# Layer 1 of a float32 network: the second matrix of three token tiles by seven block products, and the second layer's weights converted at a closer spacing

## The chip, the cores and the metric

The kernel runs on one core of one Trainium2 chip. The metric is the device time of one execution in microseconds. Before the change it is 1191.9 us, the median of three runs (1191.66 to 1201.35).

A core has these engines, each with its own in-order stream of instructions: TensorE (PE: matmuls, and loads of the stationary operand, shown as PEld), VectorE (DVE), ScalarE (ACT), GpSimd (POOL) and SyncE (SP), which here issues all DMAs. They wait for each other by semaphores. PE writes to PSUM, 8 banks of 128 partitions x 512 float32; all else lies in SBUF or, for parked data, in DRAM.

## What is computed

```python
y  = irfft(rfft(x, axis=1) * F)                 # x: 2 x 3008 x 256 -> 6016 tokens of 256
h  = y @ w_in;  x1 = (h * sigmoid(h)) @ w_out   # layer 1: 256 -> 2048 -> 256
g  = x1 @ w_gate                                # layer 2: 256 -> 1536 -> 256
out = (g * sigmoid(g) * (x1 @ w_val)) @ w_out2
```

All inputs are float32 (the weights arrive as 64-bit floats and are converted on the chip). The change touches layer 1's second product and the preparation of layer 2's weights.

## The kernel before, in words

**Split operands.** PE multiplies 128x128 blocks of weights (stationary) with up to 512 columns of data (moving). A float32 value is kept as a high and a low part, both in the type that PE takes at full rate; a product of two values is three matmuls (high x high, high x low, low x high: `PARTS`). So each operand costs an ACT cast (high) and a subtraction on DVE or POOL (low).

**Layer 1** (lines 774 to 1046) works on tiles of 512 tokens (the twelfth has 384). A *unit* is one tile t and one block f of 128 of the 2048 hidden features; there are 192, and from tile 2 on tile t holds units 16t to 16t+15. A unit does, in this order: whatever the table `todo` has for its number (weights to convert, transforms of the next tile: `s4`); `m1_in` (L527): six matmuls of 512 columns into an `h1` bank (L509), a Silu on ACT to `u` (L536), `split` (L514): high by ACT (L516), low by DVE (L517); then `drain(18)` (L1044), which issues matmuls that were queued by earlier units until 18 are left; then `m1_out` (L541), which queues this unit's six matmuls of the second matrix (L553). So the second matrix runs three units behind the first. It adds into two PSUM banks for the whole tile, and at the tile's last unit ACT copies each bank once (L559) and SP stores it to `d3`, where layer 2 reads it.

**Layer 2's weights** (`weights2`, L811): for each third q of the features and each of gate, value and output ("g", "v", "o2"), two halves are loaded and converted from 64 bits: `conv_0` (two ACT operations), `conv_a` (three on DVE: L403, L404, L407), `conv_b` (POOL, L413, 512 wide), `conv_c` (ACT high L421, POOL low L422). For "g" and "v" sums of blocks follow: `comb_a` (four POOL operations of 256 columns), `comb_b`, `comb_c` (casts on ACT, lows on POOL: L449, L454, L466, stores). Each step stands in `todo` at its own unit; `conv_c` stands one unit behind its `conv_b`. One such group starts every 11 units from unit 80 on.

**Layer 2** (`Pair`, L665) already uses seven products of blocks in place of eight, with 384 columns each, and a last matrix with 256 columns (L751) between them.

Buffers: `mp` has 35 of 4 KB, shared by nearly all; `tp` four (tile `u`); PSUM eight banks from one pool.

Of the kernel before, what the change touches and what calls it, by code (L numbers as in the profile page):

```python
# [94 lines left out]
def fft_filter_mlp_kernel(  # L95
# [681 lines left out]
    begin = {}  # L777
    for i, (l, t, _) in enumerate(units):
        begin.setdefault((l, t), i)
    todo = {}  # L780

    def at(i, fn, *args):
        todo.setdefault(i, []).append((fn, args))
# [32 lines left out]
            at(i + 8, comb_b, key, q)  # L816
            at(i + 10, comb_c, key, q)

    i = 80
    for q in range(3):  # L820
        for key in ("g", "v", "o2"):
            weights2(i, key, q)
            i += 11
    LAST = i - 3
    at(LAST, conv_s.close)

    def room():
# [274 lines left out]
```

## Time and profile before

| | |
|---|---|
| time, median of 3 runs | 1191.9 us |
| time of the profiled execution | 1192.8 us |
| its span, first to last instruction | 1191.0 us |
| granted TensorE clock | 0.998 of full speed |
| busy: PE, DVE, ACT, POOL | 1177.8, 728.0, 666.9, 432.4 us |

The page lists busy time by engine, then the chain of work that ended last, followed back from the end. Groups name the source line, the engine, the operation and the tiles (output<-inputs). Matmuls overlap: the shown length of one is longer than its distance to the next, so the cost of a matmul on PE is read from runs of equal ones, start to start. A wait is shown with what ended it.

### The profile page before, as it was taken

What the parts mean: (1) busy time and instruction counts of PE and PEld (TensorE: products, weight loads), DVE (VectorE), ACT (ScalarE), POOL (GpSimd) and SP (SyncE); (2) the same over time, 40 slices, a digit from 0 to 9 for tenths busy, and PEclk for the clock granted to TensorE, in tenths of its full rate; (3) what the DMA queues carried; (4) which work ended last, traced back from release to release, by engine and by line L of the source; (5) the groups of instructions that cost most, each with busy time, mean ns of one, the idle gap of its engine ahead of it and who ended that gap; (6) DMA issues with size and microseconds to landing.
All of it is one profiled execution on the core that took longest, in us unless ns stands there. A gap on an engine that the chain in (4) does not pass through costs nothing.

```text
span 1191.0 us, 17735 instructions
## 1 busy us (share of the span) xinstructions
PE 1177.8 (99%) x6646; PEld 1059.6 (89%) x6646; DVE 728.0 (61%) x1078; ACT 666.9 (56%) x1208; POOL 432.4 (36%) x341
## 2 busy tenths in 40 slices
PE   9899999999999999999999999999999999999998
PEld 7478788888888888888899999999999999999997
DVE  4878866763332533443345776767677676767765
ACT  4678765655565565566554454545545455454553
POOL 2547632420043244234311424334343343434332
PEclk9999999999999999999999999999999999999999
DMA  9972523323033332313573514342331434223230
GB/s 219 280 209 71 154 77 106 97 72 98 1 106 121 101 108 93 127 45 106 174 259 125 199 55 161 105 142 89 107 130 66 159 107 142 89 90 137 72 134 23
DMA packets 67574, 141.57 MB, mean 119 GB/s; under 512 B 5568, under 2 KB 32704, under 8 KB 67488
## 3 DMA queue, kind: packets, MB, share of 16 engines
q1 hardware_dynamic: 67488, 140.44, 37.0%
q8 instruction: 52, 0.85, 0.3%
q14 instruction: 34, 0.28, 0.1%
HBM read 104.50 MB, written 35.91 MB: 118 GB/s over the span
## 4 chain that ended last, share of the span: by engine, by line
PE 95%; DVE 1%; ACT 1%; DMA 1%; POOL 1%; SPq 0%; issue 0%; POOLq 0%; DVEq 0%; ACTq 0%
PE h L509 21%; PE acc L553 21%; PE acc L751 16%; PE y L616 13%; PE xa L616 8%; PE xb L616 8%; PE s L342 2%; PE s L178 2%; PE s L175 2%; DMA fr<-in_fr_dram 1%; PE s L229 1%; PE turn L247 0%; DMA zt<-d 0%; POOL w L422 0%; SPq L195 0%; POOL m L413 0%
## 5 line engine op out<-in xcount | busy, mean ns | idle before, releaser
L751 PE MATMUL acc<-w,h 128*128 128x256 f32 x1692 | 466.3, 280 | 1.9 <-DVE h L712 0.8
L751 PEld LDWEIGHTS acc<-w,h 128*128 128x128 f32 x1692 | 316.3, 188 | 3.0 <-DVE h L712 1.1
L517 DVE TENSOR_TENSOR h<-u,h 128x512 fp32r<-128x512 f32 (+1 forms) x192 | 168.6, 883 | 242.1 <-ACT h L516 241.8
L553 PE MATMUL acc<-h,w 128*128 128x512 f32 (+1 forms) x1152 | 293.2, 387 | 0.3 <-DVE h L517 0.2
L509 PE MATMUL h<-xh,w 128*128 128x512 f32 (+1 forms) x768 | 269.6, 392 | 0.6 <-POOL w L422 0.6
L553 PEld LDWEIGHTS acc<-h,w 128*128 128x128 f32 x1152 | 215.6, 188 | 44.5 <-DVE h L517 0.8
L536 ACT ACTIVATE u<-h 128x512 f32<-128x512 f32 (+1 forms) x192 | 112.6, 587 | 132.3 <-PE h L509 131.7
L616 PE MATMUL y<-xo,wst 128*128 128x384 f32 (+1 forms) x576 | 174.5, 336 | 0.0
L616 PE MATMUL xb<-xo,wst 128*128 128x384 f32 (+1 forms) x576 | 174.0, 335 | 0.0
L509 PEld LDWEIGHTS h<-xh,w 128*128 128x128 f32 x768 | 144.2, 188 | 30.2 <-POOL w L422 1.1
L616 PE MATMUL xa<-xo,w 128*128 128x384 f32 (+1 forms) x576 | 164.1, 335 | 0.0
L659 POOL TENSOR_TENSOR c<-u,s 128x384 f32<-128x384 f32 (+1 forms) x96 | 98.4, 1025 | 176.8 <-DVE u L656 138.3
L736 POOL TENSOR_TENSOR h<-c,h 128x768 fp32r<-128x768 f32 (+1 forms) x47 | 85.8, 1826 | 176.9 <-ACT h L735 173.8
L509 PE MATMUL h<-xl,w 128*128 128x512 f32 (+1 forms) x384 | 149.3, 389 | 0.0
L516 ACT CAST h<-u 128x512 fp32r<-128x512 f32 (+1 forms) x192 | 117.5, 612 | 6.2
L616 PEld LDWEIGHTS y<-xo,wst 128*128 128x128 f32 x576 | 107.3, 188 | 0.7 <-DVE u L647 0.2
L616 PEld LDWEIGHTS xb<-xo,wst 128*128 128x128 f32 x576 | 107.5, 188 | 0.0
L616 PEld LDWEIGHTS xa<-xo,w 128*128 128x128 f32 x576 | 101.5, 188 | 0.0
L709 ACT CAST h<-ga 128x768 fp32r<-128x768 f32 (+1 forms) x48 | 39.5, 823 | 100.7 <-DVE ga L707 98.4
L663 DVE TENSOR_TENSOR c<-y,s 128x384 f32<-128x384 f32 (+1 forms) x96 | 52.1, 543 | 71.4 <-PE y L616 71.4
L509 PEld LDWEIGHTS h<-xl,w 128*128 128x128 f32 x384 | 72.2, 188 | 14.7
L712 DVE TENSOR_TENSOR h<-ga,h 128x768 fp32r<-128x768 f32 (+1 forms) x47 | 70.3, 1496 | 21.4 <-ACT h L709 21.4
(104 smaller groups left out, 1493.9 us busy)
## 6 DMA issues: line engine op xcount, KB each, us to landing
wst<-ds_g SPq DMA_DIRECT2D x48, 512.0 KB, 3.5
wst<-ds_v SPq DMA_DIRECT2D x48, 512.0 KB, 3.5
raw<-in_w_out_dram SPq DMA_DIRECT2D x14, 512.0 KB, 7.8
zt<-d SPq DMA_DIRECT2D x16, 384.0 KB, 5.0
x<-in_xp_dram SPq DMA_DIRECT2D x15, 384.0 KB, 10.0
d<-z SPq DMA_DIRECT2D x11, 512.0 KB, 3.6
d<-x SPq DMA_DIRECT2D x22, 256.0 KB, 2.2
out_dram<-ob SPq DMA_DIRECT2D x21, 256.0 KB, 2.2
```

Source lines behind the costliest of these rows:

```text
L509: nc.tensor.matmul(ps[:, :n], wt[key, f // 4, g][:, wpart, o:o + P], x[xpart][:, g, :n], start=(g == 0 and k == 0), stop=(g == 1 and k == 2),)
L516: nc.scalar.copy(h[:, 0, :n], u[:, :n])
L517: nc.vector.tensor_tensor(h[:, 1, :n], u[:, :n], h[:, 0, :n], op=ALU.subtract)
L536: nc.scalar.activation(u[:, :n], ps[:, :n], AF.Silu)
L553: nc.tensor.matmul(a[:, :n], w[:, wpart, o:o + 128], h[:, xpart, :n], start=(f == 0 and k == 0), stop=(f == 15 and k == 2),)
L616: nc.tensor.matmul(o, w_op(u, key, n, wpart), x[:, xpart, :size2(t) // 2], start=(first and k == 0), stop=(last and k == 2), skip_group_ch ...
L659: nc.gpsimd.tensor_tensor(self.c[:, self.n:], u3, self.s[:, 1], op=ALU.add)
L663: nc.vector.tensor_tensor(self.c[:, :self.n], self.y, self.s[:, 0], op=ALU.add)
L709: nc.scalar.copy(h[0], a[:, :m])
L712: eng.tensor_tensor(h[1], a[:, :m], h[0], op=ALU.subtract)
L736: nc.gpsimd.tensor_tensor(h[1], c, h[0], op=ALU.subtract)
L751: nc.tensor.matmul(a[:, D * (i % 2):D * (i % 2) + D], h[hpart][:, P * i:P * i + P], w[:, wpart, f % 2], start=(at_ == 0 and k == 0 and i % ...
```

## The change

For tiles 8 to 10 (units 128 to 175; `SEVEN`) the second matrix is done pair by pair of feature blocks. A pair of two f (256 features), 256 outputs and 512 tokens is a 2x2 by 2x2 product of blocks of 128x128 with 256 columns. In place of eight block products it does seven, of sums and differences of blocks: seven times three matmuls of 256 columns, where before it was twelve of 512.

- **Weights.** `sum_a` and `sum_b` make four sums per pair (`ws1`, split into `wst`) for 8 pairs, at units 80 to 117: on POOL one operation of 512 columns, four of 128, one of 512; one ACT cast; one store to `ds1`. `load_s1` fetches a pair's 512 KB before use, 24 times.
- **Data.** `seven_in` replaces `split`. After the odd f: two differences on POOL (`t13`), two on DVE (`t24`), four casts and four lows, spread by `behind` over the three units that follow (`step2`, `step3`), so that their engines get them after the next units' own work.
- **Products.** `seven_out` queues 21 matmuls per pair; `drain(31)` at even and `drain(21)` at odd units issue 11 and 10 of them. They add into four PSUM banks: seven results of 256 columns.
- **End of a tile.** `seven_end` adds the seven results to four blocks: two copies of 256 columns on ACT, seven operations of 256 columns on DVE, two stores to `d3`.
- **Spacing.** `weights2` starts at unit 68 and every 7 units, no more at 80 and every 11, so that it ends at about unit 129. Pools open and close at other units.
- In tile 11 `drain` leaves more in the queue at first.

```diff
+SEVEN = range(8, 11)
...
         else:
             ps = psum("h1")
             mm_in(ps, "i1", f, xt_of[t], n)
+        if t in SEVEN:
+            seven_in(begin[1, t] + f, t, f, ps)
+            return
         u = tp.tile([P, 512], F32, tag="u", name="u")
...
+    def sum_a(p):
+        w = wt["o1", p // 2, p % 2].bitcast(F32)
+        s = sums1[p] = mid([P, 2, 4, P], "ws1")
+        sub = lambda o, a, b: nc.gpsimd.tensor_tensor(o, a, b, op=ALU.subtract)
+        v = s[:, 0].rearrange("p o f -> p (o f)")
+        nc.gpsimd.tensor_tensor(v, w[:, 0], w[:, 1], op=ALU.add)
+        a11, a21, a12, a22_ = (s[:, 0, i] for i in range(4))
+        nc.gpsimd.tensor_tensor(s[:, 1, 0], a21, a22_, op=ALU.add)
+        sub(s[:, 1, 1], s[:, 1, 0], a11)
+        sub(s[:, 1, 2], a11, a21)
+        sub(s[:, 1, 3], a12, s[:, 1, 1])
...
+        def step2():
+            low(x2, flat(u))
+            t24 = new("t24")
+            sub(nc.vector, t24[:, 0], u[:, 1], t13[:, 0])
+            sub(nc.vector, t24[:, 1], t24[:, 0], u[:, 0])
+            x13 = operand(5, 7, t13)
+
+            def step3():
+                low(x13, flat(t13))
+                x24 = operand(6, 4, t24)
+                behind(i + 3, low, x24, flat(t24))
+
+            behind(i + 2, step3)
+
+        behind(i + 1, step2)
...
+        block = {1: 0, 2: 2, 4: 3}
+        order = (1, 2, 5, 3, 7, 6, 4)
...
+        queue.extend((one, i, k) for i in range(7) for k in range(3))
+
+    def seven_end(t, i, a):
...
+        if i == 0:
+            nc.scalar.copy(e[:, 0], a[:, 0])
+            add(c[:, 0, 0], a[:, 1], e[:, 0])
+        elif i == 1:
+            nc.scalar.copy(e[:, 1], a[:, 0])
+            add(e[:, 2], a[:, 1], e[:, 1])
+        elif i == 2:
+            add(e[:, 0], a[:, 1], e[:, 0])
+            add(e[:, 3], a[:, 0], e[:, 0])
+            add(c[:, 0, 1], e[:, 2], e[:, 0])
+            add(c[:, 1, 1], e[:, 3], e[:, 1])
...
+        else:
+            add(c[:, 1, 0], e[:, 3], a[:, 0], ALU.subtract)
...
-    i = 80
+    i = 68
     for q in range(3):
         for key in ("g", "v", "o2"):
             weights2(i, key, q)
-            i += 11
-    LAST = i - 3
-    at(LAST, conv_s.close)
+            i += 7
+    LAST = 176
...
+    for p in range(8):
+        at(80 + 5 * p, sum_a, p)
+        at(82 + 5 * p, sum_b, p)
+    for t in SEVEN:
+        for p in range(8):
+            at(begin[1, t] + 2 * p - 4, load_s1, t, p)
...
-            m1_in(*units[i][1:])
-            drain(6 * (LAG - 1))
-            m1_out(*units[i][1:])
+            t, f = units[i][1:]
+            if t in SEVEN:
+                m1_in(t, f)
+                settle(i)
+                drain(31 if f % 2 == 0 else 21)
+                if f % 2:
+                    seven_out(t, f // 2)
+                continue
+            m1_in(t, f)
+            settle(i)
+            drain(max(6 * (LAG - 1), 33 - 6 * f) if t > SEVEN[-1] else 6 * (LAG - 1))
+            m1_out(t, f)
```

**PE, in tiles 8 and 9.** Before, every unit is six matmuls of the first matrix and six of the second (one unit of tile 8; `w` is a half of a block of weights, and a row says how many equal ones follow each other):

```order
L509 MATMUL h1_4264<-xh_3489,w_1204 128x512
L509 MATMUL h1_4264<-xl_3490,w_1204 128x512
L509 MATMUL h1_4264<-xh_3489,w_1204 128x512
L509 MATMUL h1_4264<-xh_3489,w_1267 128x512
L509 MATMUL h1_4264<-xl_3490,w_1267 128x512
L509 MATMUL h1_4264<-xh_3489,w_1267 128x512
L553 MATMUL acc_4064<-h_4179,w_1084 128x512 x3
```

Now a pair of f takes two units; six more matmuls follow behind these rows. `b11` is the high and low of the pair's first block of data, the `h` the other blocks, `w` a block of the weights, `wst` a sum of blocks, the four `acc` the four banks:

```order
L641 MATMUL acc_4336<-b11_4651,w_1402 128x256 x3
L641 MATMUL acc_4336<-h_4683,w_1402 128x256 x3
L641 MATMUL acc_4343<-h_4716,wst_4504 128x256 x3
L641 MATMUL acc_4343<-h_4683,wst_4504 128x256 x2
L512 MATMUL h1_4793<-xh_4155,w_541 128x512
L512 MATMUL h1_4793<-xl_4156,w_541 128x512
L512 MATMUL h1_4793<-xh_4155,w_541 128x512
L512 MATMUL h1_4793<-xh_4155,w_678 128x512
L512 MATMUL h1_4793<-xl_4156,w_678 128x512
L512 MATMUL h1_4793<-xh_4155,w_678 128x512
L641 MATMUL acc_4343<-h_4683,wst_4504 128x256
L641 MATMUL acc_4368<-h_4716,wst_4504 128x256 x3
```

The twelve matmuls of 512 columns of a pair have become 21 of 256, cut in two by the next unit's first matrix.

**DVE, where tile 8 ends and tile 9 begins** (units 144 to 147). Before, a tile's end has nothing on DVE; between the low halves (L517) stand only steps of the conversion:

```order
L517 TENSOR_TENSOR h_4340<-u_4338,h_4340 128x512
L517 TENSOR_TENSOR h_4362<-u_4360,h_4362 128x512
L403 TENSOR_SCALAR v2_4349<-v2_4349 128x512
L404 TENSOR_SCALAR v2_4349<-v2_4349 128x512
L407 SCALAR_TENSOR_TENSOR v2_4349<-raw_4311,v2_4349 128x512
L517 TENSOR_TENSOR h_4385<-u_4383,h_4385 128x512
L517 TENSOR_TENSOR h_4404<-u_4402,h_4404 128x512
```

Now (L577 is a low half, L595 a difference, L653 `seven_end`, `acc` a PSUM bank of tile 8, `e1` and `x2` its results):

```order
L577 TENSOR_TENSOR b11_4769<-u0_4767,b11_4769 128x256
L577 TENSOR_TENSOR h_4775<-t13_4739,h_4775 128x512
L653 TENSOR_TENSOR e1_4784<-acc_4343,e1_4784 128x256
L653 TENSOR_TENSOR e1_4784<-acc_4368,e1_4784 128x256 x2
L653 TENSOR_TENSOR x2_4785<-e1_4784 128x256 x2
L653 TENSOR_TENSOR x2_4785<-e1_4784,acc_4375 128x256
L577 TENSOR_TENSOR h_4805<-u1_4800,h_4805 128x512
L595 TENSOR_TENSOR t24_4844<-u1_4800,t13_4802 128x256
L595 TENSOR_TENSOR t24_4844<-t24_4844,u1_4800 128x256
L577 TENSOR_TENSOR h_4809<-t24_4772,h_4809 128x512
L577 TENSOR_TENSOR b11_4841<-u0_4839,b11_4841 128x256
```

Six operations of `seven_end` stand in one block ahead of the low half of `u`, the two differences `t24`, and the low half of the pair before (`t24_4772`).

**POOL, around unit 100.** Before, at units 99 to 107, these operations are all that POOL is given there (L449 and L454 `comb_b`, L466 `comb_c`, L413 `conv_b`, L422 `conv_c`):

```order
L449 TENSOR_TENSOR wa_3258<-v2_3050,wa_3258 128x512
L454 TENSOR_TENSOR wa2_2993<-v2_3050,wa2_2993 128x256
L466 TENSOR_TENSOR wst_3311<-ws_3217,wst_3311 128x4x128
L466 TENSOR_TENSOR wst_3315<-ws_3217,wst_3315 128x4x128
L413 TENSOR_TENSOR m_3319<-m_3319,e_3320 128x512
L422 TENSOR_TENSOR w_3387<-m_3319,w_3387 128x512
L413 TENSOR_TENSOR m_3391<-m_3391,e_3392 128x512
L422 TENSOR_TENSOR w_3460<-m_3391,w_3460 128x512
```

Now, at units 100 to 104 (L416 `conv_b`, L425 `conv_c`, L439 and L440 `comb_a`, L553, L555 and L557 `sum_a`, L566 `sum_b`):

```order
L416 TENSOR_TENSOR v2_3302<-v2_3302,e_3386 128x512
L555 TENSOR_TENSOR ws1_3445<-w_1092 128x512
L557 TENSOR_TENSOR ws1_3445<-ws1_3445 128x128
L553 TENSOR_TENSOR ws1_3445<-ws1_3445 128x128 x3
L425 TENSOR_TENSOR w_3471<-v2_3302,w_3471 128x512
L440 TENSOR_TENSOR ws_3496<-v2_3302 128x256
L439 TENSOR_TENSOR ws_3496<-ws_3496,v2_3302 128x256
L439 TENSOR_TENSOR ws_3496<-v2_3302 128x256
L439 TENSOR_TENSOR ws_3496<-v2_3302,ws_3496 128x256
L566 TENSOR_TENSOR wst_3505<-ws1_3445,wst_3505 128x4x128
L452 TENSOR_TENSOR wa_3550<-v2_3302,wa_3550 128x512
```

Eight operations in nine units have become thirteen in five, seven of them for the sums of layer 1's blocks; two more of units 103 and 104 follow.

## Rows read from the trace of the kernel before

**Rows 1.** The page: busy time by engine; the chain that ended last, by engine.

```profile
PE 1177.8 (99%) x6646; PEld 1059.6 (89%) x6646; DVE 728.0 (61%) x1078; ACT 666.9 (56%) x1208; POOL 432.4 (36%) x341
...
PE 95%; DVE 1%; ACT 1%; DMA 1%; POOL 1%; SPq 0%; issue 0%; POOLq 0%; DVEq 0%; ACTq 0%
```

**Rows 2.** Stretches: start:end in us, then as the header row says.

```profile
core 0: us, PE busy (x) PEld busy (x) DVE busy (x) ACT busy (x) POOL busy (x), PEclk, DMA share, GB/s
100.00:125.00 25.00, 25.00 (x109) 19.98 (x109) 21.94 (x20) 20.50 (x36) 18.46 (x11) 1.00 0.35 90
319.00:459.00 140.00, 140.00 (x644) 115.75 (x642) 57.94 (x89) 84.78 (x153) 49.19 (x43) 1.00 0.31 98
459.00:597.00 138.00, 138.00 (x632) 114.10 (x631) 52.29 (x81) 83.60 (x148) 48.81 (x42) 1.00 0.35 116
```

**Rows 3.** Timeline of PE: start us, us, instruction; runs of equal matmuls.

```profile
466.93 1.53 PE L553 MATMUL acc<-h,w 128*128 128x512 f32 x6
...
1180.61 1.48 PE L751 MATMUL acc<-w,h 128*128 128x256 f32 x11
```

**Rows 4.** Timeline of ACT: the Silu of units 80, 128 and 176.

```profile
319.43 0.60 ACT L536 ACTIVATE u<-h 128x512 f32<-128x512 f32 x1 [1.48 <-PE h L509]
...
458.97 0.60 ACT L536 ACTIVATE u<-h 128x512 f32<-128x512 f32 x1 [1.48 <-PE h L509]
...
597.31 0.49 ACT L536 ACTIVATE u<-h 128x384 f32<-128x384 f32 x1 [1.18 <-PE h L509]
```

**Rows 5.** Groups by line and form: count | busy us, mean ns | idle before.

```profile
L516 ACT CAST h<-u 128x512 fp32r<-128x512 f32 x176 | 109.3, 621 | 5.7
...
L536 ACT ACTIVATE u<-h 128x512 f32<-128x512 f32 x176 | 104.8, 595 | 117.7 <-PE h L509 117.1
...
L422 POOL TENSOR_TENSOR w<-v,w 128x512 fp32r<-128x512 f32 x12 | 15.6, 1296 | 23.0 <-ACT w L421 23.0
...
L466 POOL TENSOR_TENSOR wst<-ws,wst 128x512 fp32r<-128x512 f32 x12 | 15.3, 1293 | 24.2 <-ACT wst L465 24.2
...
L407 DVE SCALAR_TENSOR_TENSOR v<-raw,v 128x512 uint32<-128x512 uint32 x12 | 8.3, 693 | 0.4
...
L403 DVE TENSOR_SCALAR v<-v 128x512 f32<-128x512 f32 x12 | 5.0, 420 | 0.0
...
L454 POOL TENSOR_TENSOR wa<-v,wa 128x256 fp32r<-128x256 f32 x6 | 4.4, 738 | 0.0
...
L761 DVE COPY ob<-acc 128x256 f32<-128x256 f32 x3 | 1.3, 423 | 1.4 <-ACT ob L759 1.1 <-PE acc L751 0.3
...
L759 ACT COPY ob<-acc 128x256 f32<-128x256 f32 x2 | 0.7, 370 | 2.0 <-PE acc L751 2.0
```

**Rows 6.** Timeline of DVE and POOL: low halves alone, and meeting a POOL operation.

```profile
201.36 1.27 POOL L295 TENSOR_TENSOR y<-y,t2t 128x512 f32<-128x512 f32 x1 [5.15 <-DVE t2t L291]
201.76 1.42 DVE L517 TENSOR_TENSOR h<-u,h 128x512 fp32r<-128x512 f32 x1 [0.55 <-ACT h L516]
...
205.65 0.69 DVE L517 TENSOR_TENSOR h<-u,h 128x512 fp32r<-128x512 f32 x1 [0.46 <-ACT h L516]
...
481.81 2.39 DVE L517 TENSOR_TENSOR h<-u,h 128x512 fp32r<-128x512 f32 x2
482.04 1.61 POOL L413 TENSOR_TENSOR m<-m,e 128x512 uint32<-128x512 uint32 x1 [5.00 <-DVE m L407]
```

**Rows 7.** Waits of ACT from 100 to 220 us: total, times, longest.

```profile
ACT w L421 <- POOL m L413: 9.4, 6, 2.0
```

**Rows 8.** DMA issues: count, KB each, us to landing.

```profile
wst<-ds_g SPq DMA_DIRECT2D x48, 512.0 KB, 3.5
```

More of the change, by code (lines that the diff above doesn't have):

```diff
@@ L136, in fft_filter_mlp_kernel @@
     }
+    ds1 = [dr.tile([P, 1024], F32, name=f"ds1_{p}") for p in range(8)]
     dw2 = [dr.tile([P, 1024], F32, name=f"dw2_{q}") for q in range(3)]
@@ new lines, in sum_b, with load_s1, high, low @@
+    def sum_b(p):
+        c = sums1.pop(p)[:, 1]
+        w = mid([P, 4, 2, P], "wst", F32R)
+        nc.scalar.copy(w[:, :, 0], c)
+        nc.gpsimd.tensor_tensor(w[:, :, 1], c, w[:, :, 0], op=ALU.subtract)
+        store(ds1[p], w.rearrange("p o l f -> p (o l f)"))
+    def load_s1(t, p):
+        w = wt["s1", t, p] = mid([P, 4, 2, P], "wst", F32R)
+        nc.sync.dma_start(w.rearrange("p o l f -> p (o l f)").bitcast(F32), ds1[p])
+    def high(o, v):
+        nc.scalar.copy(o[:, 0], v)
+    def low(o, v):
+        nc.vector.tensor_tensor(o[:, 1], v, o[:, 0], op=ALU.subtract)
@@ new lines, in seven_in, with operand @@
+    def seven_in(i, t, f, ps):
+        p, j = divmod(f, 2)
+        new = lambda name: spp["p"].tile([P, 2, 256], F32, tag="s", name=name)
+        flat = lambda v: v.rearrange("p i n -> p (i n)")
+        u = new(f"u{j}")
+        nc.scalar.activation(flat(u), ps, AF.Silu)
+        if j == 0:
+            b11 = tp.tile([P, 512], F32, tag="u", name="b11").bitcast(F32R)
+            b11 = b11.rearrange("p (l n) -> p l n", l=2)
+            high(b11, u[:, 0])
+            hs["u"], hs[t, p] = u, {1: b11}
+            behind(i + 1, low, b11, u[:, 0])
+            return
+        u0, x = hs.pop("u"), hs[t, p]
+        sub = lambda e, o, a, b: e.tensor_tensor(o, a, b, op=ALU.subtract)
+        def operand(k0, k1, v):
+            h = mid([P, 2, 512], "h", F32R)
+            high(h, flat(v))
+            x[k0], x[k1] = h[:, :, :256], h[:, :, 256:]
+            return h
+        t13 = new("t13")
+        sub(nc.gpsimd, t13[:, 0], u0[:, 1], u0[:, 0])
+        sub(nc.gpsimd, t13[:, 1], u[:, 1], u0[:, 1])
+        x2 = operand(2, 3, u)
+        def step2():
[10 more added lines that the diff above has]
+        behind(i + 1, step2)
@@ new lines, in seven_out, with one @@
+    def seven_out(t, p):
+        w, ws = wt["o1", p // 2, p % 2], wt.pop(("s1", t, p))
+        x = hs.pop((t, p))
+        block = {1: 0, 2: 2, 4: 3}
+        order = (1, 2, 5, 3, 7, 6, 4)
+        def one(i, k):
+            n = order[i]
+            if k == 0 and p == 0 and i % 2 == 0:
+                acc[1, t, i // 2] = psum("acc")
+            a = acc[1, t, i // 2]
+            wpart, xpart = PARTS[k]
+            if n in block:
+                left = w[:, wpart, P * block[n]:P * block[n] + P]
+            else:
+                left = ws[:, {5: 0, 6: 1, 7: 2, 3: 3}[n], wpart]
+            nc.tensor.matmul(
+                a[:, 256 * (i % 2):256 * (i % 2) + 256], left, x[n][:, xpart],
+                start=(p == 0 and k == 0 and i % 2 == 0), stop=(p == 7 and k == 2),
+                skip_group_check=True,
+            )
+            if p == 7 and k == 2 and (i % 2 or i == 6):
+                seven_end(t, i // 2, a.rearrange("p (i n) -> p i n", i=2))
+        queue.extend((one, i, k) for i in range(7) for k in range(3))
@@ L779, in fft_filter_mlp_kernel, with behind @@
         begin.setdefault((l, t), i)
-    todo = {}
+    todo, post = {}, {}
+    def behind(i, fn, *args):
+        post.setdefault(i, []).append((fn, args))
     def at(i, fn, *args):
@@ L1038, in fft_filter_mlp_kernel, with settle @@
         at(1, conv_c, "o1", 0, 1)
+        def settle(i):
+            for fn, args in post.pop(i, ()):
+                fn(*args)
         for i in range(len(units)):
```

18 lines of the change are left out of this document (16 added, 2 removed).

## The prediction

> **What bounds the kernel now.** The page comes first: PE is busy 1177.8 of 1191.0 us, and 95% of the chain that ended last is PE [rows 1]. The stretches come next. From 319 to 597 us, where the change works, PE is busy all the time, DVE for about 40%, ACT for 60%, POOL for 35% [rows 2]. So PE sets the end there, and a matmul less is time saved unless PE then has to wait. Last come single operations and how they meet, which decide whether PE will wait. The unit's pace is read from the Silu: unit 80 at 319.43 us, unit 128 at 458.97, unit 176 at 597.31 [rows 4]: 2.91 and 2.88 us per unit.
>
> **Part 1: PE's saving.** A run of six matmuls of 512 columns shows 1.53 us [rows 3]. The last one's own shown length is 0.39, so the distance is (1.53 - 0.39) / 5 = 0.228 us. A run of eleven of 256 columns, each with its own weight load as in the change, shows 1.48 us with 0.28 for the last: 1.20 / 10 = 0.120 [rows 3]. A pair costs 12 x 0.228 = 2.74 us before and 21 x 0.120 = 2.52 after. The 24 pairs save 24 x 0.22 = 5.2 us. If 256 columns cost half of 512 (0.114) they would save 24 x 0.34 = 8.2; the run measured is the nearest row, so I take 5.2 and let the range go up to 6.5.
>
> **Part 2: a steady pair.** It takes 2 x 6 x 0.228 + 2.52 = 5.26 us on PE. ACT gets two Silu (0.60), four casts of 512 or less (0.62) [rows 5]: 3.7 us. DVE gets three lows of 0.69 [rows 6], one low and two differences of 256 columns. For those no row stands; 0.35 (half of 0.69) and 0.42 (256 columns out of PSUM, [rows 5]) bound them, I take 0.40. That is 3.3 us. POOL gets two differences of 256 columns at 0.74 [rows 5]. Nothing is full. The tightest operand is the low half of x24: DVE has it some 3.7 us after the pair's second Silu could start, while PE first needs it behind 10 products, a first matrix, 11 products, a first matrix and 5 products, 5.9 us. Spare: about 2 us. I cost the steady pair at nothing; its cover is that spare and the matmuls that run three units behind.
>
> **Part 3: the ends of tiles.** In unit 145 and 161 the last products of a tile are issued, and `seven_end` gives DVE a block of six operations ahead of the low half of u, the two differences and the low half of x24. Let T be the moment when PE has issued that unit's first matrix. ACT can start the Silu 0.2 us later (a matmul is shown 0.39 long at 0.23 distance), and does Silu 0.60, two casts 0.62 each, then the copy out of PSUM 0.37 [rows 5]: T + 2.4. Only then can the block start: four operations out of PSUM at 0.42, two in SBUF at 0.40, 2.5 us: T + 4.9. Then 0.69 + 0.80 + 0.69: T + 7.1. PE wants it after 10 x 0.12 + 1.37 + 11 x 0.12 + 1.37 + 5 x 0.12 = T + 5.9. PE waits 1.2 us, and two POOL differences fall into that time, each of which can hold a DVE operation up for its 0.74 (part 4): I add 0.7. So 1.9 us, twice. At the end of tile 10 the next units are ordinary ones with 384 columns, and their cast and low half stand ahead of the pair's steps: 0.2 + 0.49 [rows 4] + 0.52 + 0.55 (a cast and a low of 384 by their rows of 512, scaled a little down), then 0.69 + 0.80 + 0.69, 3.9 us, against 9 x 0.12 + 6 x 0.17 + 7 x 0.12 = 2.9 on PE: 1.0 us. Together 2 x 1.9 + 1.0 = 4.8 us; from 0 (if DVE's copies come sooner than I think) to 7.
>
> **Part 4: the weights closer together.** POOL and DVE hold each other up. A low half takes 0.69 us alone; one that starts 0.40 us into a POOL operation takes 1.42 and ends 0.55 us after that operation. The other way round, a POOL operation that starts 0.23 us into a low half takes 1.61 in place of about 1.28, and the next low half again ends 0.55 us after it [rows 6]. So one of the two works at a time, and their times add. The Trainium skill says the same ("SBUF — State Buffer", Who interferes with whom): a DVE operation with two inputs in SBUF and a GpSimd operation that reads SBUF exclude each other for a whole instruction. By the rule every operation counts in full against one budget; if the two only slowed each other a little, this part would cost nothing, as POOL alone then fits.
>
> The sum for units 76 to 125, 50 units of 2.91 = 145.5 us. By the new table POOL gets 61 operations of 512 columns at 1.29, 26 of 256 at 0.74 [rows 5], and 32 of 128 (no row; 0.46 by the straight line through the other two): 112.6 us. DVE adds 50 low halves at 0.55 and 14 `conv_a`: the last of its three operations reads two inputs (0.69 [rows 5], 0.55 held), the other two read one and count between 0 and 0.42 [rows 5]. That is 27.5 + 7.7 + 0 to 11.8. Total 147.8 to 159.6, so 2 to 14 us more than there is room for; I take 8. What is behind hangs on POOL. Its `conv_b` releases ACT's cast in `conv_c`, and behind that cast in ACT's order stand the Silu and the high half that PE needs. A unit's result is wanted three units later, 8.7 us, and its own chain takes 2 to 3 us: 5.5 to 6.5 us may be lost unseen, and 2.9 more since `conv_c` is a unit behind `conv_b`. Against this stands a stretch that is about as full: from 100 to 125 us DVE is busy 21.9 of 25, ACT 20.5, POOL 18.5, and PE all the time [rows 2]; ACT waited for POOL there 9.4 us, at most 2.0 at once [rows 7]. An overrun of 8 is just about covered, one of 14 is not. I take 2.5 us, from 0 to 10.
>
> The rest costs nothing: 24 loads and 8 stores of 512 KB are issued eight units (over 20 us) before use, against 3.5 us to landing [rows 8], and DMA is at 0.35 of its time [rows 2]; SP's queue waits for buffers that have long been read. Tile 8's first units issue only first matrices, and catch up on the queue two units later; the queue only grows. Layer 2's loads find its weights earlier in DRAM than before.
>
> **Sum.** -5.2 + 4.8 + 2.5 = +2.1 us on the profiled execution's 1192.8. That is 0.9 above the median, so against the median 1191.9 + 2.1 = 1194.0.
>
> **Rivals.**
> 1. *Everything is hidden*: DVE runs far enough ahead at the ends of tiles, and the conversion fits. Only part 1 is left: 1191.9 - 5.2 = 1186.7, down to 1185.5 with the upper saving. For it: no wait of PE shows in these 278 us, though all operands are made on the run. Against it: the block at a tile's end starts from a copy that comes after three other ACT operations.
> 2. *The conversion takes over* (the other side): POOL and DVE together become the bound in units 76 to 125, and PE follows their pace. Price: the whole overrun of 14 less some 3 that stay unseen, since each wait of ACT also delays what it would have fed; 1191.9 - 5.2 + 4.8 + 11 = 1202.5, up to 1206. It decides from an overrun of about 9 us on. For it: by single operations the sum is over the room in any case. Against it: 100 to 125 us.
> 3. *256 columns do not cost half of 512*: each product's weight load sets the distance. The break-even is 2.74 / 21 = 0.130 us. The Trainium skill speaks against the change here ("TensorE: Matmul & The Clock Gate", Back-to-back issue gap): it gives about 81 ns for 128 columns and 131 ns for 512 in a stream of loads and matmuls, by which small products are dear; by a straight line 256 would cost 98, and a pair 2.06 in place of 1.57 us. No such thing shows here: 512 columns take 0.228, 256 take 0.120. If the distance in the new runs were 0.140, a pair would lose 0.2 us, and the time be 1191.9 + 4.8 + 4.8 + 2.5 = 1204.0.
>
> **How the numbers follow.** My forecast, 1190 to 1198, has 0.60; rival 1 0.17; rival 2 0.18; rival 3 0.03; something not thought of 0.02. The predicted time is that of the first, 1194.0. The range goes from rival 1's 1186.0 to 1202.0, which takes in the lower part of rival 2 and leaves out some 0.17. A measurement of this kernel can tell about 1% from no change, 11.9 us. Faster than 1180.0 is in no case: 0.01. Slower than 1203.8 are the upper part of rival 2 and rival 3: 0.11. The rest, 0.88, is within 1%.
>
> **What would show it.** Runs of products (L641) at 0.120 us: part 1 right. PE waiting for DVE's low half (L577) about 2 us once near the start of tiles 9 and 10 and 1 us at tile 11, and at no other place in tiles 8 to 10: parts 2 and 3 right; a wait in every pair would break part 2. In units 80 to 130 POOL busy above 85%, ACT waiting for POOL in `conv_c` (L424) for several us at once, and PE short by 0 to 10 us: part 4. No wait of ACT above 3 us there would make rival 1's half of it true.

## The result and the profile after

The changed kernel took 1213.6 us (median of 6 runs, 1206.6 to 1217.1) against 1195.1 for the kernel before, measured beside it (1191.7 to 1201.4): a ratio of 1.0138, 95% interval 1.0093 to 1.0184. It is slower by about 1.4%. The forecast of 1194.0 and its range of 1186.0 to 1202.0 were wrong.

The profiled execution took 1213.7 us. Where the difference lies is read from the Silu, as in [rows 4]. These are the Silu of units 68 and 191 in the timeline of ACT, before (283.53 and 630.20 us) and after:

```profile
283.53 0.60 ACT L536 ACTIVATE u<-h 128x512 f32<-128x512 f32 x1 [0.55 <-PE h L509]
630.20 0.49 ACT L536 ACTIVATE u<-h 128x384 f32<-128x384 f32 x1 [1.07 <-PE h L509]
```

```profile
289.05 0.60 ACT L542 ACTIVATE u<-h 128x512 f32<-128x512 f32 x1 [0.55 <-PE h L512]
651.05 0.49 ACT L542 ACTIVATE u<-h 128x384 f32<-128x384 f32 x1 [1.07 <-PE h L512]
```

Before, these 123 units took 346.7 us; after, 362.0: **15.3 us more**. Layer 2 behind them takes 560.8 us in both. Ahead of them the profile after is 5.5 us late, all of it before unit 0, where the two kernels do the same: that is scatter, since unit 0's Silu lies anywhere from 71.6 to 78.7 us in the profiles of this study, at 78.7 in a kernel whose program up to there is that of before. So kernels are compared below by the time of these 123 units, beside their ratios.

The page after, busy time by engine, beside [rows 1], and the waits of PE from 280 to 640 us (what waited and for whom: total us, times, longest):

```profile
PE 1183.0 (98%) x6862; PEld 1070.3 (88%) x6862; DVE 812.6 (67%) x1195; ACT 687.5 (57%) x1264; POOL 518.2 (43%) x437
```

```profile
PE acc L641 <- DVE h L577: 5.6, 4, 1.6
PE h L512 <- DVE xl L359: 2.8, 2, 2.3
PE s L345 <- DMA zt<-d: 2.4, 2, 2.0
PE acc L687 <- DVE h L520: 2.1, 4, 1.0
PE acc L641 <- ACT h L574: 0.7, 1, 0.7
PE acc L687 <- ACT h L519: 0.4, 1, 0.4
```

The kernel before has no such line in these units. Only the first and the fifth belong to the seven products (L641); the others lie before 478 us, in the units in which the weights are converted and the sums made. Where PE loses is read from the start of each unit's first matrix in the timeline of PE. These are units 68 and 128, before and after:

```profile
281.93 0.39 PE L509 MATMUL h<-xh,w 128*128 128x512 f32 x1
457.41 0.39 PE L509 MATMUL h<-xh,w 128*128 128x512 f32 x1
```

```profile
287.46 0.39 PE L512 MATMUL h<-xh,w 128*128 128x512 f32 x1
472.50 0.39 PE L512 MATMUL h<-xh,w 128*128 128x512 f32 x1
```

So after needs 185.0 us where before needs 175.5: PE has lost 9.6 us when unit 128 begins. Read in the same way it has lost 12.2 at unit 132, and 4.2 more in units 132 and 133, which issue the products of tile 8's first pair (beside early_sums, below, whose seven products begin without any loss). The saving less the tile ends makes -1.1, as in early_sums. Together that is the 15.3.

A part of these losses is clock. After two of the long waits PE got half of its clock; the stretches (the eighth number is the granted clock, as in [rows 2]) are the one behind the wait for zt, the next one, and the one behind the waits of tile 8's first pair:

```profile
405.50:408.50 3.00, 3.00 (x8) 2.31 (x8) 2.93 (x5) 2.05 (x5) 2.29 (x2) 0.50 1.01 345
409.00:412.00 3.00, 3.00 (x15) 2.44 (x14) 0.55 (x1) 1.26 (x3) 2.27 (x3) 1.00 0.78 309
491.50:494.20 2.70, 2.70 (x10) 2.22 (x9) 2.67 (x5) 1.49 (x4) 1.29 (x1) 0.51 0.88 287
```

That is 1.2 in place of 2.4 GHz: at 406.93 us a run of six matmuls of 512 columns shows 2.42 us in place of the 1.53 of [rows 3]. It costs some 1.5 us each time, and is part of the 12.2 and of the 4.2.

**How ACT comes to stand.** The timelines of POOL, of ACT, of DVE and of PE around 350 us:

```profile
344.93 2.79 POOL L469 TENSOR_TENSOR wst<-ws,wst 128x512 fp32r<-128x512 f32 x2 [1.49 <-ACT wst L468]
347.69 1.47 POOL L555 TENSOR_TENSOR ws<-w 128x512 f32<-128x512 f32 x1
349.23 0.79 POOL L557 TENSOR_TENSOR ws<-ws 128x128 f32<-128x128 f32 x1
350.10 2.07 POOL L553 TENSOR_TENSOR ws<-ws 128x128 f32<-128x128 f32 x3
352.13 1.27 POOL L416 TENSOR_TENSOR m<-m,e 128x512 uint32<-128x512 uint32 x1
```

```profile
345.90 0.62 ACT L519 CAST h<-u 128x512 fp32r<-128x512 f32 x1
...
347.06 0.62 ACT L519 CAST h<-u 128x512 fp32r<-128x512 f32 x1
353.44 0.62 ACT L424 CAST w<-m 128x512 fp32r<-128x512 f32 x1 [5.76 <-POOL m L416]
353.96 0.62 ACT L565 CAST wst<-ws 128x512 fp32r<-128x512 f32 x1
354.49 0.59 ACT L542 ACTIVATE u<-h 128x512 f32<-128x512 f32 x1
```

```profile
345.05 1.52 DVE L406 TENSOR_SCALAR m<-m 128x512 f32<-128x512 f32 x1
346.60 1.40 DVE L407 TENSOR_SCALAR m<-m 128x512 uint32<-128x512 uint32 x1
348.04 1.67 DVE L410 SCALAR_TENSOR_TENSOR m<-raw,m 128x512 uint32<-128x512 uint32 x1
349.63 1.80 DVE L520 TENSOR_TENSOR h<-u,h 128x512 fp32r<-128x512 f32 x2
```

```profile
350.63 1.41 PE L687 MATMUL acc<-h,w 128*128 128x512 f32 x5 [0.72 <-DVE h L520]
```

ACT finishes a high half at 347.7 us and then stands at the cast of `conv_c` (L424), which needs `conv_b` (L416). DVE is done with `conv_a` at 349.7, held up itself by POOL. But POOL first makes two low halves of `comb_c` (L469) and a whole `sum_a` (L553 to L557), and comes to L416 at 352.1. (With `sum_b` a pair's sums are six operations on POOL; the section on the change says seven.) Behind the cast stands the Silu of unit 87, whose first matrix PE began at 342.58: it runs at 354.49, 11.9 us later, where before it is 1.6.

The last link to PE is mostly DVE. PE's wait at 350.63 is for the first of the two low halves at 349.63. ACT had its high half ready at 346.52, but DVE was in `conv_a` until 349.71, with three operations of 4.6 us that take 1.5 where POOL is idle. Of PE's 7.7 us of waits before 478 us, 4.9 are for DVE, 2.4 for zt and 0.4 for ACT. So here PE waits because ACT was late already and DVE, held up by POOL, added to it.

### The profile page after: what moved, and what is told of

It reads as the page before. It is cut to its first block, busy times and chain, and to the rows that moved or that the text cites. A ratio compares the mean times of both kernels' runs of the same rounds, so it can differ in the third digit from the quotient of the medians.

```text
span 1211.9 us, 18548 instructions
## 1 busy us (share of the span) xinstructions
PE 1183.0 (98%) x6862; PEld 1070.3 (88%) x6862; DVE 812.6 (67%) x1195; ACT 687.5 (57%) x1264; POOL 518.2 (43%) x437
## 4 chain that ended last, share of the span: by engine, by line
PE 58%; DVE 2%; POOL 2%; issue 1%; ACT 1%; POOLq 0%; DVEq 0%
PE acc L885 16%; PE y L750 12%; PE xa L750 8%; PE xb L750 8%; PE h L512 6%; PE acc L641 4%; PE acc L687 2%; PE s L345 1%; DVE h L577 0%; POOL w L425 0%; POOL m L416 0%; DVE h L520 0%; DVE x L653 0%; POOL wst L566 0%; POOL v L416 0%
## 5 line engine op out<-in xcount | busy, mean ns | idle before, releaser
L520 DVE TENSOR_TENSOR h<-u,h 128x512 fp32r<-128x512 f32 (+1 forms) x144 | 143.7, 1008 | 138.7 <-ACT h L519 133.7
L687 PE MATMUL acc<-h,w 128*128 128x512 f32 (+1 forms) x864 | 221.8, 387 | 2.9 <-DVE h L520 2.4
L687 PEld LDWEIGHTS acc<-h,w 128*128 128x128 f32 x864 | 161.9, 189 | 38.1 <-DVE h L520 4.9
L542 ACT ACTIVATE u<-h 128x512 f32<-128x512 f32 (+1 forms) x144 | 83.9, 582 | 47.1 <-PE h L512 45.0
L519 ACT CAST h<-u 128x512 fp32r<-128x512 f32 (+1 forms) x144 | 87.7, 609 | 4.6
```

The lines of the kernel that those rows point to most:

```text
L519: nc.scalar.copy(h[:, 0, :n], u[:, :n])
L520: nc.vector.tensor_tensor(h[:, 1, :n], u[:, :n], h[:, 0, :n], op=ALU.subtract)
L687: nc.tensor.matmul(a[:, :n], w[:, wpart, o:o + 128], h[:, xpart, :n], start=(f == 0 and k == 0), stop=(f == 15 and k == 2),)
```

## The experiments

All ratios are to the kernel before on the same chip. The table puts together what the sections below read: the time of units 68 to 191 against the 346.7 of before; what PE has lost by the start of unit 128; then, in the stretch from the Silu of unit 76 to that of unit 126 (its ends in whole us), its length, the busy time of POOL and of ACT, and ACT's waits for anybody but PE (the view of waits, summed), all in us.

| kernel | ratio [95%] | 68 to 191 | by 128 | length | POOL | ACT | ACT's waits |
|---|---|---|---|---|---|---|---|
| before | | 0 | 0 | 148 | 48.5 | 89.3 | 11.2 |
| after | 1.0138 [1.0093, 1.0184] | +15.3 | 9.6 | 164 | 130.4 | 103.0 | 59.2 |
| close_alone | 0.9999 [0.9983, 1.0015] | 0.0 | 0.0 | 147 | 86.1 | 100.0 | 30.9 |
| close_and_sums | 1.0087 [1.0062, 1.0111] | +10.0 | 8.9 | 163 | 131.0 | 103.6 | 57.6 |
| no_unused_split | 0.9997 [0.9981, 1.0014] | -1.1 | 0.0 | 147 | 118.3 | 98.9 | 27.7 |
| no_unused_pool | 1.0077 [1.0054, 1.0101] | +8.6 | 3.9 | 157 | 118.7 | 102.4 | 52.8 |
| no_unused_act | 1.0053 [1.0035, 1.0072] | +5.3 | 1.8 | 154 | 130.9 | 98.3 | 48.5 |
| early_zt | 1.0121 [1.0096, 1.0147] | +14.4 | 9.1 | 163 | 130.7 | 102.7 | 58.6 |
| early_sums | 0.9995 [0.9973, 1.0018] | -1.1 | 0.0 | 147 | 86.0 | 100.1 | 28.6 |
| later_cast | 1.0104 [1.0075, 1.0132] | +12.3 | 7.2 | 162 | 135.9 | 102.6 | 53.9 |
| half_sums | 1.0052 [1.0032, 1.0073] | +7.0 | 2.7 | 157 | 110.3 | 100.8 | 52.7 |
| sums_on_dve | 0.9997 [0.9976, 1.0018] | +1.0 | 0.6 | 151 | 103.0 | 103.1 | 41.7 |

### Which part of the change costs the time

**wide_again**, the old spacing put back:

```diff
-    i = 68
+    i = 80
-            i += 7
+            i += 11
```

> The changed kernel with only the old spacing of the second layer's weights put back (unit 80, step 11); sums of weights and seven products stay. Theory (POOL and DVE have more work in units 76 to 125 than the stretch is long, and PE is held through it): POOL's 9 conversions spread over 99 units again, so the overrun goes; left are the saving of 5.8 us and the tile ends of 4.5 us: 0.995 to 1.003 of the kernel before. Rival A (the seven products themselves cost the time): stays at 1.010 to 1.018. Rival B (the start before unit 0 was really made slower by the change, 5.5 us in its profile): Silu of unit 0 at 77 to 79 us here too.

Measured: 1.0170 [1.0148, 1.0191]; units 68 to 191 take 22.3 us more. The theory's forecast fell, and the number lies in rival A's range. Up to unit 128 nothing is lost (Silu of unit 68 to that of 128: 175.4 us, as before), as the theory says; but the conversion now runs through tiles 8 to 10, and there PE waits in many pairs for the operands of the seven products (waits of PE, 280 to 640 us):

```profile
PE acc L641 <- DVE h L577: 19.9, 17, 2.6
```

So the spare 2 us of a steady pair hold only while POOL and DVE have no conversion to do: the closer spacing is not an extra of this change but what its products need. That they cost the time by themselves, as rival A has it, falls with early_sums below, which keeps them and loses nothing. Rival B fell too: unit 0's Silu is at 71.6 us here.

**close_alone**, the kernel before with the closer spacing alone:

```diff
-    i = 80
+    i = 68
-            i += 11
+            i += 7
-    LAST = i - 3
+    LAST = 176
```

> The kernel before with only the spacing changed (unit 68, step 7); no sums of weights, no seven products. Theory: without the sums POOL and DVE have some 36 us less to do in units 76 to 125 (147.8 to 159.6 becomes about 112 to 123 against 145.5 us of room), so nothing is late: 0.999 to 1.003. Rival A: the same, 1.000. Rival C (the spacing alone does it, by ACT's casts or SP's queue of loads and stores): 1.007 or more.

Measured: 0.9999 [0.9983, 1.0015], and no wait of PE in these units. The closer spacing by itself is free.

**close_and_sums**, the changed kernel with no tile computed by seven products:

```diff
-SEVEN = range(8, 11)
+SEVEN = range(0)
...
-            drain(max(6 * (LAG - 1), 33 - 6 * f) if t > SEVEN[-1] else 6 * (LAG - 1))
+            drain(6 * (LAG - 1))
```

> The changed kernel with its seven products taken out: units of tiles 8 to 10 as before, weights at step 7, and the sums of weights made and stored but read by nobody. Theory: the overrun in units 76 to 125 is all there and the saving is not: 1.008 to 1.014, the waits of PE at the same places as in the changed kernel between 349 and 475 us, some 10 to 12 us of them. Rival A: 0.999 to 1.003, PE without such waits.

Measured: 1.0087 [1.0062, 1.0111], +10.0 us, as the theory had it, with PE's starts too far apart at the places of the kernel after (by 0.85 us at 347.8, 1.14 at 391.1, 1.86 at 399.0, 0.89 at 470.2, and half clock from 403.6 on). (The 24 loads of the sums, from unit 124 on, are left out here too.) So the sums in units 80 to 117, with the conversions, cost about 10 of the 15.3 us. The seven products add 5.4 to that: -1.1 for their saving less the tile ends, 4.2 at the first pair of tile 8, which ACT and DVE enter late, and 2.3 close ahead of it (the last wait for xl is 2.5 us at 472.5 in the kernel after, 0.9 here).

**no_unused_split.** The trace of ACT's waits led to `conv_c`: for g and v nobody reads what it makes.

```diff
         v, _ = parts.pop((key, q, half))
+        if key in ("g", "v"):
+            return
```

> The changed kernel without conv_c for the keys g and v: 12 casts on ACT and 12 low halves on POOL whose results nobody reads (comb_b splits the same numbers again). Theory: POOL has 12 x 1.29 = 15.5 us less in units 76 to 125, 132 to 144 against 145.5 us of room, the overrun goes: 0.995 to 1.003 of the kernel before, ACT's waits for POOL in conv_c under 2 us each. Rival A: 1.010 to 1.018, the waits in conv_c gone without PE getting faster.

Measured: 0.9997 [0.9981, 1.0014], units 68 to 191 1.1 us faster than before. The expected -1.3 (-5.8 + 4.5) is nearly there and PE waits at the tile ends alone. One expectation was wrong: ACT still stands in `conv_c` (L426, for o2) for more than 2 us three times, once for 5.8, and PE doesn't notice.

### What reaches PE

The theory so far was that of the prediction: POOL and DVE together have more to do than fits. Seven more kernels put it to the test.

**early_sums**, the sums where POOL has room:

```diff
-        at(80 + 5 * p, sum_a, p)
-        at(82 + 5 * p, sum_b, p)
+        at(30 + 6 * p, sum_a, p)
+        at(32 + 6 * p, sum_b, p)
```

> The changed kernel with the sums of weights moved from units 80 to 117 to units 30 to 74 (a step of 6), where the traces of before show POOL and the two-input operations of DVE at about half of the time together. Theory: 147.8 to 159.6 us in units 76 to 125 falls by the 36 us of the sums, so the overrun goes and the saving of 5.8 us less the 4.5 us at tile ends is left: 0.995 to 1.001. Rival A (the seven products themselves cost it): 1.010 or more.

Measured: 0.9995 [0.9973, 1.0018], -1.1 us; as expected.

**no_unused_pool**: in `conv_c` only POOL's subtraction is left out for g and v.

```diff
-        nc.gpsimd.tensor_tensor(w[:, 1], v, w[:, 0], op=ALU.subtract)
+        if key not in ("g", "v"):
+            nc.gpsimd.tensor_tensor(w[:, 1], v, w[:, 0], op=ALU.subtract)
```

> The changed kernel without the 12 low halves that conv_c makes on POOL for g and v (nobody reads them); the 12 casts on ACT ahead of them stay, with their waits for conv_b. Theory (one budget of POOL and DVE is overdrawn): 15.5 us of 147.8 to 159.6 gone from POOL, 0.997 to 1.003 of the kernel before. Rival D (ACT's own work and its order are what holds PE: 12 casts of 0.62 us and their waits): little of it comes back, 1.007 or more.

Measured: 1.0077 [1.0054, 1.0101], +8.6 us. The theory's 0.997 to 1.003 fell. POOL is busy for 118.7 us in the stretch, as in no_unused_split (118.3), which loses nothing. What differs is ACT. These are ACT's waits in that stretch, here and without the whole unread split:

```profile
ACT w L424 <- POOL v L416: 20.9, 9, 4.8
ACT w L424 <- POOL m L416: 13.8, 5, 5.7
```

```profile
ACT w L426 <- POOL m L416: 11.8, 4, 5.8
```

**no_unused_act**: only the cast on ACT is left out, and POOL subtracts v from itself.

```diff
-        nc.scalar.copy(w[:, 0], v)
-        nc.gpsimd.tensor_tensor(w[:, 1], v, w[:, 0], op=ALU.subtract)
+        if key not in ("g", "v"):
+            nc.scalar.copy(w[:, 0], v)
+        nc.gpsimd.tensor_tensor(w[:, 1], v, w[:, 0] if key not in ("g", "v") else v, op=ALU.subtract)
```

> The changed kernel with only the 12 casts on ACT left out in conv_c for g and v; POOL makes a difference of the same size from the same numbers (of no use to anybody), so POOL has as much to do as in the changed kernel, but ACT no longer waits there for POOL (9 waits, 21.0 us, up to 5.2). Theory with ACT as the path on which POOL's lateness reaches PE: nearly as good as without both, 0.998 to 1.004. Theory with other paths (xl of the next tile on DVE, zt behind stores in SP's queue, POOL's backlog at the start of tile 8): 1.008 or more, PE's waits at the same places.

Measured: 1.0053 [1.0035, 1.0072], +5.3 us, between both expectations: with POOL as busy as after (130.9 us) ten of the 15.3 us come back when ACT does not stand at those casts. By unit 128 the loss is 1.8 in place of 9.6 us; at tile 8's first pair 4.7 us are lost, where the kernel after loses 4.2. Of ACT's other waits 18.9 us are for raw weights, 13.9 for o2's `conv_b`, 7.1 for xl and 5.9 for the sums' `ws`.

**early_zt**, zt of tiles 6 to 11 loaded earlier:

```diff
-                at(i - 10, load_zt, c // 4)
+                at(i - (16 if t > 5 else 10), load_zt, c // 4)
```

> The changed kernel with zt of tiles 6 to 11 loaded 16 units ahead in place of 10. If SP's in-order queue behind stores that wait for POOL is one path among several: the wait of s4 for zt (2.2 us at 400.8) and the stretch at half clock behind it (about 2 us) go, 1.008 to 1.012. If it is the main path: 1.004 or less. If zt's lateness only shows what another wait would show anyway: no change, 1.012 to 1.016.

Measured: 1.0121 [1.0096, 1.0147], +14.4 us. The wait for zt is gone, and in its place PE waits 2.1 us at 401.2 for a low half (L520), with half clock behind it as before. SP's queue was late, but hardly later than ACT and DVE.

**later_cast**, nothing taken away, the casts two units later:

```diff
-                at(max(i + k, 0), fn, key, q, half)
+                at(max(i + k + (2 if k == 2 and key in ("g", "v", "o2") else 0), 0), fn, key, q, half)
```

> The changed kernel with conv_c of the second layer's weights two units later (three units behind conv_b in place of one): same operations and the same sizes on every engine, only the place of 18 casts in ACT's order (and of what follows them) is another. Theory O (order: PE is held because ACT's in-order queue stands at these casts while POOL is late with conv_b, up to 5.8 us at once): 0.999 to 1.005, ACT's waits for POOL in conv_c under 2 us each. Theory B (budget: POOL and DVE have more to do than fits into units 76 to 125): 1.009 or more, since nothing is taken away.

Measured: 1.0104 [1.0075, 1.0132], +12.3 us. Theory O fell. Theory B's range was met, but half_sums and sums_on_dve below speak against B. ACT no longer stands at these casts, but, from 280 to 500 us, at the raw weights (30.1 us), at the sums' `ws` (8.7) and at xl (9.1). In the stretch of the table its waits sum to 53.9 us in place of 59.2. To move a wait is little help while the work behind it is as late.

**half_sums**, every second sum moved ahead, and **sums_on_dve**, the five operations of `sum_a` on DVE, were to tell an edge in POOL's amount of work from the length of POOL's queue:

```diff
-        at(80 + 5 * p, sum_a, p)
-        at(82 + 5 * p, sum_b, p)
+        at(30 + 6 * p if p % 2 == 0 else 80 + 5 * p, sum_a, p)
+        at(32 + 6 * p if p % 2 == 0 else 82 + 5 * p, sum_b, p)
```

> The changed kernel with every second sum of weights (p even) moved ahead, to units 30 to 68; four stay in units 85 to 117. In the traces so far POOL is busy in units 76 to 125 for 130 us with all eight sums and 86 with none, so about 108 here, below the 118 of the kernel without the unread splits, which lost nothing. Theory B1 (how much POOL and DVE have to do in these units decides, with an edge near 118): 0.997 to 1.002. Theory Q (no edge: each piece of POOL work that stands ahead of conv_b in POOL's queue makes ACT's cast late, and with the 12 unread casts still there ACT is held): between, 1.004 to 1.008.

```diff
-        nc.gpsimd.tensor_tensor(v, w[:, 0], w[:, 1], op=ALU.add)
+        nc.vector.tensor_tensor(v, w[:, 0], w[:, 1], op=ALU.add)
...
```

> The changed kernel with the five operations of sum_a on DVE in place of POOL, at the same places in the order (sum_b stays). POOL loses 40 operations in units 80 to 115, some 25 us of its 130, and its queue ahead of conv_b gets shorter; on DVE the same work is about half as long, so the two together fall by some 12 us only. Theory Q (POOL's queue ahead of conv_b): 0.998 to 1.003. If the common time of POOL and DVE decides: the sum falls less than in the kernel without the 12 unread low halves on POOL (15.5 us), which stood at 1.008, so 1.006 to 1.010; DVE's low halves of h then come later than in the changed kernel.

Measured: half_sums 1.0052 [1.0032, 1.0073], +7.0 us; sums_on_dve 0.9997 [0.9976, 1.0018], +1.0. Both as theory Q said. POOL is busy for 110 us in half_sums, less than in no_unused_split, and still 7 us are lost: no edge in POOL's amount. In sums_on_dve POOL and DVE together are busy for 222 us of 151, as in the kernel after (222 of 164), and PE loses one us. (A shown time includes what one engine holds up in the other.) Nor does the work taken away order the losses: by the expectations 12 us less leave a loss of 1.0 us (sums_on_dve), 15.5 less leave 8.6 (no_unused_pool). So their common time is not what decides.

What orders the losses by unit 128 is ACT's time: its work plus its waits for others than PE. The stretch in the kernel after, in early_sums and in sums_on_dve (fourth busy time: ACT):

```profile
313.00:477.00 164.00, 156.24 (x699) 125.89 (x698) 91.82 (x105) 103.05 (x192) 130.41 (x120) 0.99 0.49 167
```

```profile
310.00:457.00 147.00, 147.00 (x678) 121.57 (x677) 83.29 (x105) 100.10 (x184) 85.97 (x72) 1.00 0.47 158
```

```profile
311.00:462.00 151.00, 150.66 (x693) 124.22 (x692) 118.93 (x145) 103.12 (x193) 103.00 (x80) 1.00 0.53 181
```

And ACT's waits in it after, all of them:

```profile
ACT w L424 <- POOL v L416: 21.0, 9, 5.2
ACT w L424 <- POOL m L416: 14.2, 4, 5.8
ACT xh L358 <- DVE xl L359: 9.1, 4, 3.4
ACT wst L565 <- POOL ws L553: 7.0, 5, 4.0
ACT m L400 <- DMA raw<-in_w_out_dram: 6.6, 3, 4.5
ACT v L400 <- DMA raw<-in_w_gate_dram: 1.3, 1, 1.3
```

After, 103.0 + 59.2 = 162.2 of 164 us: ACT waits for PE at no time, it has no slack left. PE's own pace would need 147. In the kernels with a sum up to 130.9 (before 100.5, close_alone 130.9, early_sums 128.7, no_unused_split 126.6) PE loses nothing by unit 128. Then the loss rises with the sum: 0.6 us at 144.8 (sums_on_dve), 1.8 at 146.8 (no_unused_act), 2.7 at 153.5 (half_sums), 3.9 at 155.2 (no_unused_pool), 7.2 at 156.5 (later_cast), and 8.9 to 9.6 at 161.2 to 162.2. This is a reading of the traces, not an experiment of its own. Where ACT never waits for PE the sum is nearly the stretch's length by itself, so it says that ACT is late, not why. No run added work to ACT alone, and a wait shrinks when work is put ahead of it.

The loss at tile 8's first pair goes by how late ACT still is there. In the kernels in which the Silu of unit 132 comes 3.6 to 4.3 us later behind its first matrix than before (after, early_zt, no_unused_pool, no_unused_act) it is 4.2 to 4.9 us; with 2.1 and 2.2 (half_sums, sums_on_dve) it is 1.4 and 1.5; in early_sums, where the Silu is in time, it is nothing.

### A kernel that keeps the gain

**before_no_unused**, the kernel before without the unread split (the diff of no_unused_split), tells whether that is worth anything by itself:

> The kernel before without conv_c for g and v. PE has no wait in these units that could go away, so by either theory nothing changes: 0.998 to 1.002.

Measured: 0.9994 [0.9972, 1.0015]. It is not.

**early_no_unused** has early_sums and no_unused_split together:

> The changed kernel with the sums in units 30 to 74 and without conv_c for g and v. PE is free of waits but for the tile ends with the sums moved alone, so nothing more is gained: 0.997 to 1.001, the saving of 5.8 us less 4.5 us at the tile ends.

Measured: 0.9995 [0.9976, 1.0014], -1.1 us in units 68 to 191; as expected.

**deferred_end** adds to that the tile ends:

```diff
-                seven_end(t, i // 2, a.rearrange("p (i n) -> p i n", i=2))
+                behind(now1[0] + 1, seven_end, t, i // 2, a.rearrange("p (i n) -> p i n", i=2))
...
+            now1[0] = i
             t, f = units[i][1:]
...
+            if t > SEVEN[-1]:
+                settle(i)
             m1_in(t, f)
             settle(i)
```

> As early_no_unused, and the six operations of seven_end are issued one unit later, behind the low half of x24; in tile 11 the steps of the last pair go ahead of the unit's own split. Theory: the waits of 1.75, 1.76 and 0.94 us at the tile ends go and the whole saving of 5.8 us is left: 0.994 to 0.997. If banks of PSUM that are read later hold up the next tile's first products: 0.998 to 1.003, with PE waiting there for a bank.

Measured: 0.9975 [0.9954, 0.9996], 1191.9 against 1194.7 us; units 68 to 191 take 341.5 us, 5.2 less than before, and PE has no wait from 280 to 640 us. It is the one kernel here that is faster than before, by a quarter of a per cent, and its interval only just leaves out no change; the expected 0.994 to 0.997 lies in the lower part of the interval, and the 5.2 us of the trace would be 0.9956.

## Why the prediction was wrong

- **Part 1, right.** Seven products in a row:

```profile
504.90 0.99 PE L641 MATMUL acc<-h,wst 128*128 128x256 f32 x7
```

  (0.99 - 0.28) / 6 = 0.118 us apart; the median over the tiles is 0.119, so the 24 pairs save 24 x (2.74 - 2.50) = 5.8 us, inside 5.2 to 6.5. deferred_end, in which PE waits nowhere in these units, is 5.2 us shorter than before: the predicted figure. Rival 3 fell with it.

- **Part 2, right with its cover, and the cover is POOL.** In the kernel after no steady pair waits but the first of tile 8. wide_again shows what it costs when conversion takes POOL and DVE: 17 waits in place of four (three of the four are the tile ends). The prediction named the spare 2 us, not that the closer spacing keeps them free.

- **Part 3, right.** PE waits at the starts of tiles 9 and 10 for the low half of x24, and once at tile 11 (timeline of PE, tile 9):

```profile
539.31 0.75 PE L641 MATMUL acc<-h,wst 128*128 128x256 f32 x5
541.65 0.51 PE L641 MATMUL acc<-h,wst 128*128 128x256 f32 x2 [1.59 <-DVE h L577]
```

  DVE's block of six and what followed it:

```profile
536.31 1.21 DVE L653 TENSOR_TENSOR e<-acc,e 128x256 f32<-128x256 f32 x3 [1.56 <-ACT e L661]
537.44 1.29 DVE L653 TENSOR_TENSOR x<-e 128x256 f32<-128x256 f32 x2
538.66 0.41 DVE L653 TENSOR_TENSOR x<-e,acc 128x256 f32<-128x256 f32 x1
538.99 0.68 DVE L577 TENSOR_TENSOR h<-u,h 128x512 fp32r<-128x512 f32 x1
539.59 0.41 DVE L595 TENSOR_TENSOR t<-u,t 128x256 f32<-128x256 f32 x1
540.04 0.42 DVE L595 TENSOR_TENSOR t<-t,u 128x256 f32<-128x256 f32 x1
540.38 1.22 DVE L577 TENSOR_TENSOR h<-t,h 128x512 fp32r<-128x512 f32 x1
```

  PE's starts lie 1.75, 1.76 and 0.94 us too far apart, where 1.9, 1.9 and 1.0 were predicted. The units were named wrongly: the last products of a tile run in units 146 and 147, not 145. deferred_end takes these waits away by the order alone; it is 4.0 us faster in these units than early_no_unused (341.5 against 345.5 us), where the sum of this part was 4.8.

- **Part 4 is the step that failed: 2.5 us were taken, at most 10, and PE lost 12.2 before tile 8's first pair.** One of its signs was there (waits of ACT in `conv_c` of several us at once); another was not (POOL busy for 130.4 of 164 us, 80%, where above 85% was named). Rival 2 had the outcome right, that the conversion takes over; its 1202.5 to 1206, 10.6 to 14 us more than before, is a little under the 15.3 of the trace. Its bound, POOL and DVE together, was wrong too. Two things in the step were wrong. First the account: it added POOL's and DVE's time and set an overrun of 8 us against what may be lost unseen. half_sums, no_unused_pool and sums_on_dve show that this sum does not decide. In its place the traces show ACT's time running out, 89.3 us of work and 11.2 of waits before, 103.0 and 59.2 after. Of the 59.2, 42.2 are for POOL. That ACT is the path is shown in part: no_unused_act, with POOL as busy as after, loses 1.8 in place of 9.6 us by unit 128.

  Secondly the size. The slack was not taken too large: "5.5 to 6.5 us may be lost unseen", and 2.9 more. In no_unused_pool the Silu of unit 88 stands 8.1 us further behind its first matrix than before, and PE does not wait. no_unused_split has one wait of 5.8 us and loses nothing. But the lateness was not 8 us: from the Silu of unit 76 to that of unit 126 ACT needs 164.1 us after and 147.2 before, 16.9 more. Some 7 of these stay unseen, and 9.6 are lost on PE by unit 128. The waits came about every 10 us (18 for POOL in 164 us), and ACT had no time between them to catch up. The stretch taken as "about as full" was as busy [rows 2], but it is 25 us long, and ACT's 9.4 us [rows 7] are 6 waits in 120 us, from 100 to 220.

- **"The rest costs nothing" failed in two places.** SP's queue did not only wait for buffers: it stood behind stores of what POOL had yet to make, 56 us for the sums' `wst` in L446 alone from 325 to 500 us, and PE waited 2.4 us for zt. By early_zt that costs about 1 us, as DVE's low half was late at the same place. And tile 8's first pair, taken as free, lost 4.2 us, since ACT and DVE came into it late and the clock fell; in early_sums and no_unused_split, where they do not, it loses nothing.

- The sum by the terms that were measured: -5.2 + 4.0 + 12.2 + 4.2 = +15.2 of the 15.3 us, where the prediction had -5.2 + 4.8 + 2.5 = +2.1.

Open stays how the 59 us of waits divide between POOL's queue and chains that go to and fro between ACT, DVE and POOL, and how much of PE's loss DVE adds by itself. Either half of the unread split alone gives back much of the loss by unit 128 (5.7 of 9.6 us without POOL's subtraction, 7.8 without ACT's cast), but nothing at tile 8's first pair; both together give back all.

## What to carry to other kernels

Where engines feed each other in order, add up for each one its work and its expected waits over the whole stretch, and compare that with the pace of the engine that sets the end; slack of a few units pays for one late operand, not for one in every third unit. The waits themselves came from traces here; before a run they can only be guessed from the queue of the helper. When side work is packed closer, look at what stands ahead, in the helper's queue, of the operation for which a busy engine will stand; moving eight sums to a stretch where POOL had room, or removing 24 operations that nobody read, each gave back all that was lost. Before pricing such work, ask whether its results are read at all.

## What the runs showed of the hardware

A DVE operation with one input in SBUF can be held up by POOL as well. `tensor_scalar` on 512 columns takes 0.41 to 0.43 us alone; at 345.05 and 346.60 us, in the timeline above, it took 1.52 and 1.40, while POOL was at work without a break. The prediction counted these between 0 and 0.42. The Trainium skill has this rule ("SBUF — State Buffer", Who interferes with whom): `tensor_scalar` can run in a mode that uses both ports and then excludes GpSimd for the whole instruction. This trace agrees.

PE's waits of 2.0 and 0.5 us (at 401 to 404) and of 0.7 and 1.6 us (at 488 to 491) were followed by some 3 us at half clock, 0.50 and 0.51; the waits of 2.5 us at 472.5 and of 1.75 us at the tile ends were not. In half_sums the wait for xl at the place of the 2.5 us, 2.2 us long, was. What tells them apart the runs don't show; it made a late operand dearer by about 1.5 us each time.
